# Talking-heads attention with a PReLU layer pair: larger matmul tiles for scores and products, and spaced rows in the relay

## The chip, the cores and the metric

The kernel runs on one core of one Trainium2 chip. The metric is the time of one execution on the device in microseconds (us); lower is better.

## The reference

Four batches, 12 heads, 448 positions, head size 64. The scores are mixed over the heads before the softmax and the weights after it; the result, laid out as 1,792 rows of 768, goes through two dense layers with a PReLU between them. The layers' weights come in as float64.

```python
scores = scale * np.matmul(q, k.transpose(0, 1, 3, 2))
scores = np.einsum('bhij,hg->bgij', scores, w_pre)
attn = np.exp(scores - np.max(scores, axis=-1, keepdims=True))
attn = attn / (np.sum(attn, axis=-1, keepdims=True) + 1e-09)
attn = np.einsum('bhij,hg->bgij', attn, w_post)
x = np.matmul(attn, v)            # then (b, i) rows of 12 x 64
h = x @ w_in
g = np.maximum(h, 0.0) + alpha * np.minimum(h, 0.0)
return g @ w_out
```

## The kernel before

There are two stages. Stage 1 is the attention of all batches; beside it the float64 weights are rounded to float32 on VectorE (`convert`, lines 51 to 57) and stored to memory (`wsc`). Stage 2 (from line 394 on) is the two dense layers: `l1` (line 435) and `l2` (line 460).

In stage 1 the 448 query rows of a batch are cut into four chunks of 110, 110, 110 and 118 rows. A chunk's rows are cut into groups of ten, `GI`, so that ten rows times 12 heads fill 120 partitions; there are 45 groups in a batch and 180 in all. The last group of a 118-row chunk begins two rows early. Two groups make a step `m`; there are 90 steps.

The path of a chunk: `qk` (line 147) computes the scores of two heads, one from the upper and one from the lower 64 rows of the array, on up to 64 query rows at a time, for the six pairs `p` of heads; `qk_out` (line 155) copies them to `s_t`, with the query rows on the partitions and (head, key) along them. `relay` (line 162) is a DMA for each group, on chip: it takes ten rows of `s_t` and lays their 120 (row, head) pairs on 120 partitions of `sr`. `mix` (line 170) multiplies by the pre-softmax weights, `rmax` (175), `exp` (182) and `norm` (188 to 192) make the softmax, and `post` (line 204) applies the post-softmax weights and turns the result, so that keys are on the partitions; `post_out` (214) copies it to `a_t`. When all groups of a chunk are there, `pv` (line 226) multiplies with v, in units of six heads, `hx` 0 and 1. It takes the keys in blocks of 64, seven of them: even blocks from partitions 0 to 63 and odd ones from 64 to 127, each into a PSUM bank of its own, and `pv_out` (235, 236) copies one bank on ScalarE and adds the other on VectorE. The sum is stored to `x2` in memory.

The order on each engine is written out by hand in `step(m)`: the loads that are due, mix(m+1), the stores put off from the step before, the relays (up to those of pair m+4), norm(m-1), rmax(m+1), exp(m), the first `qk` or `pv` unit of this step with its copy, post(m-2), the other units, some of the conversion's operations. [...] Relays are issued in turn from SP and GpSimd. The list `jobs` says at which steps the `qk` and `pv` units and the loads stand, from the groups' numbers. `qk` and `pv` share one PSUM buffer (`ps_s`), `post` has one of its own (`pa`), which is zeroed at the start, and `mix` has two. `sr` has eight buffers, `s_t` two.

Of the kernel before, what the change touches and what calls it, by code (L numbers as in the profile page):

```python
# [14 lines left out]
ALU = mybir.AluOpType  # L15
# [4 lines left out]
B, H, S, D = 4, 12, 448, 64  # L20
DM, DFF = 768, 2048
NT = B * S
GI = 10
GP = GI * H
HI = GI // 2
HP = HI * H
CHUNKS = [(0, 110), (110, 110), (220, 110), (330, 118)]
CW = 118
NCC = DM // 128
NFC = DFF // 128  # L30
NP = H // 2
NS = 4
NJ = S // 64
SR0 = 4
# [26 lines left out]
def talking_heads_prelu(ctx: ExitStack, tc: tile.TileContext, q, k, v, w_pre, w_post, mask, w_in, w_out, alpha, out):  # L61
    nc = tc.nc
# [5 lines left out]
    groups, first = [], []  # L68
    chunk_list = [(b, c) for b in range(B) for c in range(len(CHUNKS))]
    for ci, (b, c) in enumerate(chunk_list):  # L70
        first.append(len(groups))
        cn = CHUNKS[c][1]
        for r in range(0, cn, GI):
            groups.append((ci, min(r, cn - GI)))
    NG, NC = len(groups), len(chunk_list)
    NB = NG // 2
    first.append(NG)
# [34 lines left out]
    k_t, q_t, v_t, s_t, a_t = {}, {}, {}, {}, {}  # L112
# [9 lines left out]
    def load_q(ci, dmas=None):  # L122
        b, c = chunk_list[ci]
        c0, cn = CHUNKS[c]
        q_t[ci] = qp.tile([128, NP, CW], F32, tag="q", name=f"q{ci}")
        for hf in range(2):
            dma = dmas[hf] if dmas else nc.gpsimd
            dma.dma_start(out=q_t[ci][64 * hf:64 * hf + 64, :, :cn],
                          in_=q[b, :, H * c0 + NP * hf * cn:H * c0 + NP * (hf + 1) * cn])

    def load_v(b):
        v_t[b] = vp.tile([128, NS, DM], F32, tag="v", name=f"v{b}")
        nf = S // 128
        nc.gpsimd.dma_start(out=v_t[b][:, :nf, :], in_=v[b, :nf * 128].rearrange("(s p) n -> p s n", p=128))
        nc.gpsimd.dma_start(out=v_t[b][:S - nf * 128, nf, :], in_=v[b, nf * 128:])

    u_t = {}

    def qk(ci, p, ps_pool=None):
        b, c = chunk_list[ci]  # L140
        cn = CHUNKS[c][1]
        ps = (ps_pool or ps_s).tile([128, 2, 512], F32, tag="m" if ps_pool else "s", name=f"s{ci}_{p}")
        for lo in range(0, cn, 64):
            hi = min(lo + 64, cn)
            for hf in range(2):
                r = slice(64 * hf, 64 * hf + 64)
                nc.tensor.matmul(ps[lo:hi, hf, :S], q_t[ci][r, p, lo:hi], k_t[b][r, p, :], start=True, stop=True)  # L147
        u_t["qk", ci, p] = ps

    def qk_out(ci, p, copy=nc.scalar.copy):  # L150
        cn = CHUNKS[chunk_list[ci][1]][1]
        if p == 0:
            s_t[ci] = sp.tile([CW, H, S], F32, tag="s", name=f"st{ci}")
        dst = s_t[ci].rearrange("p (t n) s -> p n t s", t=2)
        copy(dst[:cn, p], u_t.pop(("qk", ci, p))[:cn, :, :S])  # L155

    sr_t, m_t, nm_t, e_t, se_t, r_t = {}, {}, {}, {}, {}, {}

    def relay(n, dma):
        ci, r = groups[n]  # L160
        sr_t[n] = sr_b[n % NSR]
        dma.dma_start(out=sr_t[n][SR0:SR0 + GP], in_=s_t[ci][r:r + GI])  # L162

    def mix(m):

# [41 lines left out]
    def post_out(m):  # L207
        for g in range(2):
            n = 2 * m + g
            ci, r = groups[n]  # L210
            if n == first[ci]:
                a_t[ci] = ap_.tile([128, NS, H, CW], F32, tag="a", name=f"at{ci}")
            dst = a_t[ci].rearrange("p s h i -> p (s h) i")[:, :, r:r + GI]
            nc.scalar.copy(dst, pa[:, g, :NS * GP].rearrange("p (s i) -> p s i", i=GI))  # L214

    def pv(ci, hx, ps_pool=None):
        b, c = chunk_list[ci]
        cn = CHUNKS[c][1]
        ps = (ps_pool or ps_s).tile([128, 2, 512], F32, tag="m" if ps_pool else "s", name=f"x{ci}_{hx}")
        for cl in range(3):  # L220
            for s in range(NS):
                for t in range(2):
                    h = 2 * (3 * hx + cl) + t
                    for r in range(2 if 2 * s + 1 < NJ else 1):
                        pr = slice(64 * r, 64 * r + 64)
                        nc.tensor.matmul(ps[64 * t:64 * t + 64, r, cl * CW:cl * CW + cn], v_t[b][pr, s, h * D:(h + 1) * D],  # L226
                                         a_t[ci][pr, s, h, :cn], start=(s == 0), stop=(2 * s + 2 + r >= NJ))
        u_t["pv", ci, hx] = ps

    def pv_out(ci, hx):  # L230
        b, c = chunk_list[ci]
        c0, cn = CHUNKS[c]
        xe = xep.tile([128, 3, CW], F32, tag="xe", name=f"xe{ci}_{hx}")
        src = u_t.pop(("pv", ci, hx))[:, :, :3 * CW].rearrange("p r (c i) -> p r c i", c=3)
        nc.scalar.copy(xe[:, :, :cn], src[:, 0, :, :cn])
        nc.vector.tensor_tensor(xe[:, :, :cn], src[:, 1, :, :cn], xe[:, :, :cn], ALU.add)  # L236
        later.append(lambda: nc.sync.dma_start(
            out=x2[3 * hx:3 * hx + 3, :, b * S + c0:b * S + c0 + cn].rearrange("c p i -> p c i"), in_=xe[:, :, :cn]))

# [32 lines left out]
    for ci, (b, c) in enumerate(chunk_list):  # L272
        if ci:
            m0, m1 = first[ci - 1] // 2 - RAHEAD, first[ci] // 2 - RAHEAD - 2
            for p in range(NP):
                at(max(m0 + p * (m1 - m0) // (NP - 1), p // 2), "qk", ci, p)
        if ci >= 2:
            at(max(first[ci - 2] // 2 - 1, 0), "load", load_q, ci)
        if c == 0:
            if b:  # L280
                at(first[ci] // 2 - 15, "load", load_k, b)
            at(first[ci] // 2 + 3 if b else 1, "load", load_v, b)
        lb = (first[ci + 1] - 1) // 2
        at(lb + LAG + 1, "pv", ci, 0)
        at(lb + LAG + (3 if ci + 1 < NC else 1), "pv", ci, 1)
    conv_steps = NFC * 2 * 7

    with tc.manual_schedule():
        p0 = ExitStack()
        start = p0.enter_context(tc.tile_pool(name="start", bufs=1))  # L290
        hw = (nc.sync, nc.scalar)
        load_q(0, hw)
        load_k(0, ((0, 1), (1, 3), (3, 6)), hw)

# [18 lines left out]
        for i, w in enumerate((w_pre, w_post)):  # L313
            for p in ((SR0, 64), (0, 64))[i]:
                nc.gpsimd.dma_start(out=mask_sb[p:p + HP, i], in_=mask[:HP, :HI, :])
                nc.gpsimd.dma_start(out=wb[p:p + HP, i, :],
                                    in_=w.rearrange("(o h) g -> o h g", o=1).to_broadcast([HI, H, H]))
        load_q(1)
        nc.gpsimd.dma_start(out=alpha_sb, in_=alpha)
        conv = convert()  # L320
        next(conv)
        nc.vector.scalar_tensor_tensor(
            out=wk[:, :HP].rearrange("p (i g) -> p i g", g=H), in0=mask_sb[:, 0], scalar=scale,
# [4 lines left out]
            out=wq.rearrange("p g i -> p i g"), in0=mask_sb[:, 1],  # L328
# [3 lines left out]
        for p in range(NP):  # L332
            qk(0, p, None if p % 3 == 2 else ps_m)
            qk_out(0, p, nc.vector.tensor_copy if p % 2 else nc.scalar.copy)
# [3 lines left out]
        def relays(upto, dmas):  # L338
            nonlocal relayed
            while relayed < min(upto, NG):  # L340
                relay(relayed, dmas[relayed % len(dmas)])
                relayed += 1

        relays(2 * (RAHEAD + 1), (nc.sync, nc.scalar, nc.gpsimd))
        done = 0
        live = lambda m: 0 <= m < NB
        EV = {"qk": (qk, qk_out), "pv": (pv, pv_out)}

        def step(m):
# [23 lines left out]
            if live(m - LAG):  # L373
                post(m - LAG)
                post_out(m - LAG)
# [52 lines left out]
        def l1(u):  # L428
            b, f = divmod(u, NFC)
            w, x = wi_t.pop(u), xs_t[b]  # L430
            ps = P2["h"].tile([128, 512], F32, tag="h", name=f"h{u}")
            i = 0
            for cc in range(NCC):
                for tw, tx in ((0, 0), (0, 1), (1, 0)):
                    nc.tensor.matmul(ps[:, :S], w[:, tw, cc * 128:(cc + 1) * 128], x[:, tx, cc, :],  # L435
                                     start=(i == 0), stop=(i == 3 * NCC - 1))
                    i += 1
            return ps
# [39 lines left out]
        for u in range(NU + 1):  # L478
            b, f = divmod(u, NFC)
# [4 lines left out]
            if u < NU:  # L484
                split_w(u, 1)
                ps = l1(u)
# [44 lines left out]
```

## Time and profile before

| | us |
|---|---|
| median of 3 runs | 1038.42 |
| lowest, highest | 1031.63, 1039.06 |
| profiled execution, first to last instruction | 1038.9 |

The profiled execution has its span alone; what lies around it is not shown apart. Stage 1 ends, and stage 2 begins, between 540 and 560 us of the span. Rows of the trace begin with a line number of the kernel, the engine and the operation; `out<-in` are the tiles by the program's names: `s` the scores in PSUM, `st` in SBUF, `sr` the relayed rows, `m` the mix, `pa` the output of post, `at` its copy, `x` the products with v, `xe` their copy. Each float32 matmul of the source stands as two in the trace, each with a weight load.

### The profile page before, as it was taken

The page shows a single profiled execution, that of the slowest core. Times are in us where ns is not written, and L with a number is a line of the kernel's source. Part 1 is how long each engine was busy: PE and PEld are TensorE (multiplying, and loading weights), DVE is VectorE, ACT ScalarE, POOL GpSimd, SP SyncE. Part 2 cuts the span into 40 slices and gives each one's busy share as a digit, 9 for nine tenths or more (in the row PEclk, how much of TensorE's full clock was granted, in tenths as well). Part 3 has the DMA queues.
Part 4 walks back from the last instruction along what each step waited for, and adds up shares of the span by engine and source line. Part 5 has one row for each costly group of instructions (what it writes and reads, how often), then busy time and mean ns, then how long its engine had stood idle before and what let it go on. Part 6 is the DMA issues. An engine that isn't in the chain of part 4 may idle for free.

```text
span 1038.9 us, 26286 instructions
## 1 busy us (share of the span) xinstructions
PE 869.1 (84%) x11540; PEld 687.8 (66%) x11540; DVE 500.2 (48%) x886; ACT 441.6 (43%) x870; POOL 348.7 (34%) x305
## 2 busy tenths in 40 slices
PE   4656767867868687778666999999999999999998
PEld 2134444544535355455455999999999999999997
DVE  3454666656657376758624224632265224542222
ACT  1453666655657466648342232323233323232322
POOL 3121222222212122211004455554455454545452
PEclk9687898988889798889796999999999999999999
DMA  7698878897899977898618600020001000010001
GB/s 149 154 185 193 173 190 204 220 220 179 167 228 213 200 191 181 186 247 176 145 32 316 271 1 19 1 89 1 1 19 63 27 1 9 9 54 1 1 1 53
DMA packets 55209, 123.86 MB, mean 119 GB/s; under 512 B 21080, under 2 KB 38840, under 8 KB 54712
## 3 DMA queue, kind: packets, MB, share of 16 engines
q0 software_dynamic: 15232, 59.01, 25.7%
q1 hardware_dynamic: 38546, 60.12, 20.7%
q10 hardware_dynamic: 1318, 3.08, 1.2%
q8 instruction: 90, 1.47, 0.6%
q14 instruction: 23, 0.19, 0.1%
HBM read 59.85 MB, written 23.59 MB: 80 GB/s over the span
## 4 chain that ended last, share of the span: by engine, by line
PE 67%; DMA 16%; ACT 7%; issue 5%; DVE 4%; SPq 1%; POOL 0%; ACTq 0%; DVEq 0%; POOLq 0%
PE h L435 23%; PE acc L460 23%; DMA sr<-st 14%; PE s L147 7%; PE x L226 6%; PE m L170 4%; PE pa L204 4%; ACT st L155 3%; ACT at L214 2%; ACT e L182 1%; DMA xr<-x 1%; DMA wb<-in_w_post_dram 1%; DMA cr<-in_w_out_dram 1%; DVE xe L236 1%; DVE nm L175 1%
## 5 line engine op out<-in xcount | busy, mean ns | idle before, releaser
L435 PE MATMUL h<-xs,wi 128*128 128x448 f32 x1152 | 251.4, 371 | 12.6 <-DVE xs L425 11.3
L460 PE MATMUL acc<-g,wo 128*128 128x448 f32 x1152 | 248.2, 368 | 0.0
L435 PEld LDWEIGHTS h<-xs,wi 128*128 128x128 f32 x1152 | 218.4, 190 | 35.4 <-issue 11.5
L460 PEld LDWEIGHTS acc<-g,wo 128*128 128x128 f32 x1152 | 216.2, 188 | 21.8
L413 POOL TENSOR_TENSOR wi<-wr,wi 128x768 fp32r<-128x768 f32 x64 | 118.6, 1853 | 269.8 <-ACT wi L412 269.8
L204 PEld LDWEIGHTS pa<-r,e 64*64 64x64 f32 x5040 | 115.4, 146 | 79.6 <-issue 55.4
L175 DVE TENSOR_REDUCE nm<-m 128x2 f32<-128x896 f32 x90 | 97.9, 1088 | 135.7 <-PE m L170 135.5
L444 DVE TENSOR_SCALAR t<-h,alpha_sb 128x448 f32<-128x448 f32 x64 | 43.8, 684 | 245.7 <-PE h L435 245.7
L204 PE MATMUL pa<-r,e 64*64 64x60 f32 x5040 | 121.9, 234 | 43.6 <-issue 33.8
L170 PE MATMUL m<-sr,wk 64*64 64x448 f32 (+1 forms) x720 | 111.6, 650 | 50.4 <-DMA sr<-st 43.2
L446 ACT CAST g<-t 128x448 fp32r<-128x448 f32 x64 | 36.3, 567 | 275.2 <-DVE t L445 275.2
L162 POOL DMA_DIRECT2D sr<-st x88 | 54.2, 617 | 276.9 <-PE m L170 185.0
L147 PE MATMUL s<-k,q 64*46 64x448 f32 (+2 forms) x768 | 112.7, 640 | 39.5 <-ACT st L155 27.8
L214 ACT COPY at<-pa 128x480 f32<-128x480 f32 x180 | 93.2, 572 | 82.2 <-PE pa L204 82.0
L413 POOL TENSOR_TENSOR wo<-wr,wo 128x768 fp32r<-128x768 f32 x64 | 123.8, 1935 | 7.6 <-ACT wo L412 5.9
L182 ACT ACTIVATE e<-m,nm 128x448 f32<-128x448 f32 x180 | 113.7, 646 | 14.2 <-DVE nm L175 14.2
L226 PEld LDWEIGHTS x<-at,v 64*64 64x64 f32 x2688 | 88.2, 146 | 37.6 <-issue 20.3
L155 ACT COPY st<-s 110x896 f32<-110x896 f32 (+1 forms) x93 | 84.6, 909 | 63.0 <-PE s L147 55.6
L226 PE MATMUL x<-at,v 64*64 64x110 f32 (+1 forms) x2688 | 92.6, 280 | 18.5 <-issue 13.3
L147 PEld LDWEIGHTS s<-k,q 64*64 64x64 f32 (+2 forms) x768 | 27.5, 140 | 92.3 <-ACT st L155 70.9
L170 PEld LDWEIGHTS m<-sr,wk 64*64 64x64 f32 (+1 forms) x720 | 29.3, 151 | 77.5 <-issue 64.7
L412 ACT CAST wo<-wr 128x768 fp32r<-128x768 f32 x64 | 53.8, 841 | 62.3 <-PE acc L460 62.3
(46 smaller groups left out, 564.1 us busy)
## 6 DMA issues: line engine op xcount, KB each, us to landing
sr<-st SPq DMA_DIRECT2D x89, 210.0 KB
sr<-st POOLq DMA_DIRECT2D x88, 210.0 KB, 9.7
cr<-in_w_in_dram POOLq DMA_DIRECT2D x16, 768.0 KB, 11.5
cr<-in_w_out_dram POOLq DMA_DIRECT2D x16, 768.0 KB, 10.1
wsc<-ct SPq DMA_DIRECT2D x32, 384.0 KB
wr<-wsc SPq DMA_DIRECT2D x14, 768.0 KB
xr<-x SPq DMA_DIRECT2D x24, 224.0 KB
out_dram<-o SPq DMA_DIRECT2D x24, 224.0 KB
```

The costliest lines, as they stand in the source:

```text
L147: nc.tensor.matmul(ps[lo:hi, hf, :S], q_t[ci][r, p, lo:hi], k_t[b][r, p, :], start=True, stop=True)
L155: copy(dst[:cn, p], u_t.pop(("qk", ci, p))[:cn, :, :S])
L162: dma.dma_start(out=sr_t[n][SR0:SR0 + GP], in_=s_t[ci][r:r + GI])
L170: nc.tensor.matmul(ps[hf:hf + 64, u, :S], wk[r, :], g[r, :], start=True, stop=True)
L175: nc.vector.tensor_reduce(out=nm, in_=m_t[m][:, :, :S], axis=AX.X, op=ALU.max, negate=True)
L182: nc.scalar.activation(out=e_t[m][:, u], in_=m_t[m][:, u, :S], func=AF.Exp, bias=nm_t[m][:, u:u + 1], scale=1.0, accum_out=se_t[m][:, u:u ...
L204: nc.tensor.matmul(dst[:, :, HI * u:HI * u + HI], e[h, u, 64 * jb:64 * jb + 64], r[h, u].rearrange("p (h i) -> p h i", h=H), start=True, s ...
L214: nc.scalar.copy(dst, pa[:, g, :NS * GP].rearrange("p (s i) -> p s i", i=GI))
L226: nc.tensor.matmul(ps[64 * t:64 * t + 64, r, cl * CW:cl * CW + cn], v_t[b][pr, s, h * D:(h + 1) * D], a_t[ci][pr, s, h, :cn], start=(s == ...
L413: nc.gpsimd.tensor_tensor(t[:, 1], w, t[:, 0], ALU.subtract)
L435: nc.tensor.matmul(ps[:, :S], w[:, tw, cc * 128:(cc + 1) * 128], x[:, tx, cc, :], start=(i == 0), stop=(i == 3 * NCC - 1))
L460: nc.tensor.matmul(accs[c][:, :S], w[:, tw, c * 128:(c + 1) * 128], g[:, tg], start=(f == 0 and i == 0), stop=(f == NFC - 1 and i == 2))
```

## The change

The chunks are now 120, 120, 120 and 90 rows, the last of which begins at row 358, so that rows 358 and 359 of a batch are in two chunks. A chunk has 12 or 9 whole groups, 45 in a batch as before. A group's ten rows are no longer neighbours: group `r` takes every 12th (9th) row from row `r` on, and writes its ten columns of `a_t` side by side, so that `a_t`'s columns are in the order of the groups. `qk` takes all 120 (90) rows of a chunk in one tile of 64 rows and 128 columns. `pv` takes 128 keys at a time in tiles of 128 rows and 64 columns, four times, into one PSUM bank; the upper half of the last 128 is not there, and v is zero-filled for it (`a_t` has zeros there already). `pv_out` is now three copies on one engine, ScalarE for `hx` 0 and VectorE for `hx` 1, which put the columns back in the order of the rows.

```diff
-CHUNKS = [(0, 110), (110, 110), (220, 110), (330, 118)]
-CW = 118
+CHUNKS = [(0, 120), (120, 120), (240, 120), (358, 90)]
+CW = 120
+QOFF = [H * sum(n for _, n in CHUNKS[:c]) for c in range(len(CHUNKS))]
...
-        cn = CHUNKS[c][1]
-        for r in range(0, cn, GI):
-            groups.append((ci, min(r, cn - GI)))
+        groups += [(ci, r) for r in range(CHUNKS[c][1] // GI)]
...
         nf = S // 128
+        nc.gpsimd.memset(v_t[b][64:, nf, :], 0.0)
...
-        for lo in range(0, cn, 64):
-            hi = min(lo + 64, cn)
-            for hf in range(2):
-                r = slice(64 * hf, 64 * hf + 64)
-                nc.tensor.matmul(ps[lo:hi, hf, :S], q_t[ci][r, p, lo:hi], k_t[b][r, p, :], start=True, stop=True)
+        for hf in range(2):
+            r = slice(64 * hf, 64 * hf + 64)
+            nc.tensor.matmul(ps[:cn, hf, :S], q_t[ci][r, p, :cn], k_t[b][r, p, :], start=True, stop=True)
...
-        dma.dma_start(out=sr_t[n][SR0:SR0 + GP], in_=s_t[ci][r:r + GI])
+        dma.dma_start(out=sr_t[n][SR0:SR0 + GP], in_=s_t[ci][r:CHUNKS[chunk_list[ci][1]][1]:CHUNKS[chunk_list[ci][1]][1] // GI])
...
-            dst = a_t[ci].rearrange("p s h i -> p (s h) i")[:, :, r:r + GI]
+            dst = a_t[ci].rearrange("p s h i -> p (s h) i")[:, :, GI * r:GI * r + GI]
...
-                    for r in range(2 if 2 * s + 1 < NJ else 1):
-                        pr = slice(64 * r, 64 * r + 64)
-                        nc.tensor.matmul(ps[64 * t:64 * t + 64, r, cl * CW:cl * CW + cn], v_t[b][pr, s, h * D:(h + 1) * D],
-                                         a_t[ci][pr, s, h, :cn], start=(s == 0), stop=(2 * s + 2 + r >= NJ))
+                    nc.tensor.matmul(ps[64 * t:64 * t + 64, 0, cl * CW:cl * CW + cn], v_t[b][:, s, h * D:(h + 1) * D],
+                                     a_t[ci][:, s, h, :cn], start=(s == 0), stop=(s == NS - 1))
...
-        src = u_t.pop(("pv", ci, hx))[:, :, :3 * CW].rearrange("p r (c i) -> p r c i", c=3)
-        nc.scalar.copy(xe[:, :, :cn], src[:, 0, :, :cn])
-        nc.vector.tensor_tensor(xe[:, :, :cn], src[:, 1, :, :cn], xe[:, :, :cn], ALU.add)
+        ps = u_t.pop(("pv", ci, hx))
+        copy = nc.vector.tensor_copy if hx else nc.scalar.copy
+        for cl in range(3):
+            copy(xe[:, cl, :cn].rearrange("p (k g) -> p g k", k=GI),
+                 ps[:, 0, cl * CW:cl * CW + cn].rearrange("p (g k) -> p g k", k=GI))
```

The load of q takes its offsets from `QOFF`, since the chunks of q, as laid out for the loads, hold 450 rows a batch.

## Rows read from the trace of the kernel before

**Rows 1.** Stretches: us, busy us (instructions) by engine, granted clock, DMA share, GB/s.

```profile
40.00:520.00 480.00, 352.61 (x8561) 229.47 (x8555) 298.01 (x591) 280.95 (x630) 94.05 (x153) 0.87 0.84 192
540.00:1038.00 498.00, 482.07 (x2388) 437.07 (x2388) 184.31 (x254) 143.16 (x205) 242.17 (x128) 0.98 0.14 50
320.00:360.00 40.00, 28.35 (x675) 17.88 (x669) 23.12 (x48) 20.78 (x46) 7.17 (x12) 0.83 0.98 204
400.00:440.00 40.00, 32.88 (x776) 21.99 (x772) 25.47 (x50) 23.11 (x50) 10.00 (x17) 0.85 0.76 185
160.00:200.00 40.00, 30.06 (x799) 20.20 (x794) 26.08 (x53) 24.70 (x56) 8.87 (x14) 0.91 0.87 221
```

**Rows 2.** The page's chain that ended last, by line, shares of the span.

```profile
PE h L435 23%; PE acc L460 23%; DMA sr<-st 14%; PE s L147 7%; PE x L226 6%; PE m L170 4%; PE pa L204 4%; ACT st L155 3%; ACT at L214 2%; ACT e L182 1%; DMA xr<-x 1%; DMA wb<-in_w_post_dram 1%; DMA cr<-in_w_out_dram 1%; DVE xe L236 1%; DVE nm L175 1%
```

**Rows 3.** The waits of TensorE: us in total, times, longest us.

```profile
PE m L170 <- DMA sr<-st: 43.2, 11, 9.7
PE pa L204 <- issue: 33.8, 14, 6.2
PE s L147 <- ACT st L155: 27.8, 34, 3.2
PE x L226 <- issue: 13.3, 6, 4.9
...
PE m L170 <- issue: 6.2, 2, 3.8
```

**Rows 4.** TensorE in order of time: start, us, ..., [idle before <- releaser].

```profile
14.40 1.72 PE L147 MATMUL s<-k,q 64*64 64x448 f32 x16 [1.31 <-DVE st L155]
16.05 1.27 PE L301 MATMUL warm<-warm 128*128 128x448 f32 x5
...
27.60 3.25 PE L170 MATMUL m<-sr,wk 64*64 64x448 f32 x12 [9.68 <-DMA sr<-st]
33.78 1.01 PE L170 MATMUL m<-sr,wk 64*64 64x448 f32 x2 [2.93 <-DMA sr<-st]
...
359.84 0.40 PE L204 MATMUL pa<-r,e 64*64 64x60 f32 x13 [3.12 <-issue]
...
462.02 0.98 PE L170 MATMUL m<-sr,wk 64*64 64x448 f32 x8 [2.56 <-DMA sr<-st]
462.79 3.98 PE L226 MATMUL x<-at,v 64*64 64x110 f32 x81
...
497.41 1.77 PE L170 MATMUL m<-sr,wk 64*64 64x448 f32 x8 [5.78 <-DMA sr<-st]
...
523.87 2.33 PE L226 MATMUL x<-at,v 64*64 64x110 f32 x81
```

**Rows 5.** The DMA view from 40 to 520 us: all packets, and the instruction queue.

```profile
DMA packets 40872, 92.19 MB, mean 192 GB/s; under 512 B 17077, under 2 KB 27511, under 8 KB 40405
...
q8 instruction: 68, 1.11, 1.0%
```

**Rows 6.** The DMA view from 404.2 to 406.6 us.

```profile
DMA packets 156, 0.25 MB, mean 106 GB/s; under 512 B 17, under 2 KB 152, under 8 KB 156
```

**Rows 7.** The DMA view from 570 to 585 us.

```profile
DMA packets 1337, 6.23 MB, mean 415 GB/s; under 512 B 144, under 2 KB 400, under 8 KB 1336
```

**Rows 8.** Line 162's view: GpSimd's relays, from issue to landing.

```profile
DMA to landing us min/median/max: 5.3/9.7/21.7
```

**Rows 9.** The page's engines, and groups of instructions, shapes kept apart for the copies.

```profile
PE 869.1 (84%) x11540; PEld 687.8 (66%) x11540; DVE 500.2 (48%) x886; ACT 441.6 (43%) x870; POOL 348.7 (34%) x305
...
L147 PE MATMUL s<-k,q 64*46 64x448 f32 (+2 forms) x768 | 112.7, 640 | 39.5 <-ACT st L155 27.8
...
L226 PE MATMUL x<-at,v 64*64 64x110 f32 (+1 forms) x2688 | 92.6, 280 | 18.5 <-issue 13.3
...
L236 DVE TENSOR_TENSOR xe<-x,xe 128x330 f32<-128x330 f32 x24 | 12.0, 500 | 40.6 <-ACT xe L235 40.5
L235 ACT COPY xe<-x 128x330 f32<-128x330 f32 x24 | 10.4, 435 | 53.0 <-PE x L226 53.0
```

More of the change, by code (lines that the diff above doesn't have):

```diff
@@ L128, in load_q @@
             dma.dma_start(out=q_t[ci][64 * hf:64 * hf + 64, :, :cn],
-                          in_=q[b, :, H * c0 + NP * hf * cn:H * c0 + NP * (hf + 1) * cn])
+                          in_=q[b, :, QOFF[c] + NP * hf * cn:QOFF[c] + NP * (hf + 1) * cn])
     def load_v(b):
```

## The prediction

> **What bounds the kernel now.** I took the slowest core's time by stage first, then what each stage waits for, then the transfers behind those waits. The views by stretch [rows 1] split the run in two. From 540 us on TensorE is busy 482 of 498 us at a granted clock of 0.98, in the matmuls of lines 435 and 460, which the diff doesn't touch; the chain of work [rows 2] has 46% of the span there. So everything happens in the first 540 us, and nothing that the change does can give more than that stage has to give.
>
> From 40 to 520 us TensorE is busy 352.6 of 480 us, at a mean clock of 0.87, while the 16 DMA engines are busy 0.84 of the time and yet move only 192 GB/s [rows 1]. The 127 us in which TensorE stands still are told apart by the table of waits [rows 3]: 43.2 us for a relay (the DMA of line 162, s_t to sr) to land, 33.8 + 13.3 + 6.2 = 53.3 us under "issue", in which the profile shows no semaphore that it waited for, and 27.8 us for ScalarE to free the scores' PSUM buffer. VectorE (298 us) and ScalarE (281 us) have slack [rows 1]. The chain gives the relays 14% of the span, the largest share of anything in this stage [rows 2]. So the first stage is TensorE's, held up by transfers.
>
> The "issue" waits I read as late instruction fetches. They break into the middle of a run of post's matmuls, as the 3.12 us at 359.84 [rows 4]; the instruction queue has 68 packets from 40 to 520 us [rows 5], so they would come to 0.8 us a packet; and they are largest where the DMA engines are fullest: the stretch 320 to 360 has a share of 0.98 and that wait is in it, the stretch 400 to 440 has 0.76 and none [rows 1].
>
> **The relay's rate.** Around 405 us one relay runs with almost nothing beside it. It moves 106 GB/s [rows 6]. The same engines move 415 GB/s in the weights' loads of stage 2 [rows 7]: 26 GB/s each. A relay takes ten rows of s_t, so ten engines at that rate would move 260 GB/s. 210 KB are 215,040 B: 2.0 us at the rate shown, 0.83 us at the other, so 1.2 us lie in how it is read or written. The destination is 120 neighbouring partitions before and after; only the source changes, from ten neighbouring partitions to ten that are 12 or 9 apart. The trace alone can't say that the source is the slow side; I take it at the full 1.2 us, between 0 and that, because the destination is spread as widely as that of the fast load. [...]
>
> **The sum, part by part**, against the profiled execution's own span of 1038.9 us, which is 0.5 us over the median of the runs, so no correction is made.
>
> Relay waits. From issue to landing a relay takes 5.3 us at best and 9.7 in the median [rows 8]; the 4.4 between are queueing, mostly behind other relays. With 0.83 for 2.0 us the best becomes 4.1 and the queueing 4.4 x 0.83 / 2.0 = 1.8, together 5.9: every relay lands 3.8 us earlier. Two of the waits are the start's, 9.68 and 2.93 us, with eight relays at once; I leave 5 of the 12.6. The other 30.6 are single waits such as 2.56 and 5.78 us [rows 4], which 3.8 us cover nearly; I leave 3. So 43.2 becomes 8: -35 us (bounds -43 and 0).
>
> Fetch waits. A unit of scores goes from 4 matmuls in the source to 2, one of v's products from 42 to 24. The trace counts two for each: 768 and 2688 become 384 and 1536 [rows 9]. Ahead of stage 2 stand 9,216 matmuls (11,540 less stage 2's 2 x 1,152 and the warm-up's 20), so 1,536 of them go, with as many weight loads: 17%. By count alone the 53.3 us lose 9. With a share of DMA time nearer to 0.65 (92 MB [rows 5] at 415 GB/s would need 222 us, 0.54 of some 410) most fetches come in time: I leave 15, so -38 us (bounds -9 and -53).
>
> Clock. Stalls are followed by work at the lower level: a mix (line 170) takes 1.77 us after the wait at 497.41 and 0.98 at 462.02, and v's products take 3.98 us at 462.79 and 2.33 at 523.87 [rows 4]. I take the mean clock from 0.87 to the 0.91 of the stretch 160 to 200 [rows 1]: 352.6 x (1 - 0.87/0.91) = 15.5 us, of which TensorE's busy share, 0.73, lies on the path: -11 (bounds 0, and -29 at stage 2's 0.98).
>
> Streaming: nothing. Four 64x64 tiles ran side by side, now two larger ones do. Scores: 448 columns by two passes either way, 0.86 us a unit where two stand back to back (1.72 us at 14.40) [rows 4]. v's products: 12 rounds of two either way, 2.33 us for 110 columns; the columns are 450 for 448 in a batch.
>
> Changes of tile shape. All of the stage had 64-row, 64-column tiles; now 96 score units and 32 product units stand between mixes and posts that keep them, so up to 2 x 128 = 256 changes. Between tiles of one shape the next matmul starts 0.21 us ahead of the last one's end (462.02 + 0.98 against 462.79). At the one change of shape in the trace, scores to the warm-up at 16.05, it starts 0.07 ahead of 14.40 + 1.72 [rows 4]. So a change costs between 0 and 0.14 us: 0 to 36. I take half, 18, times 0.73: +13. [...]
>
> Output copies. Before, ScalarE copied one half (435 ns) and VectorE added the other (500 ns) for every unit [rows 9]. Now one engine makes three copies of a third of the columns with a stride in the output, each between 0 and 435 or 500 ns: at most 1.3 us on ScalarE for 16 units (+0.9 each, 14 us) and 1.5 us on VectorE for 16, against what they did for 32. Both have 180 us of slack, and VectorE no longer waits for ScalarE's half. The store that waits for them stands ahead of the relays in SP's queue, as before. If that cover is gone it costs those 14 us; I take 0.
>
> The rest: the memset of v's last half block stands ahead of v's loads and the next relay on GpSimd's queue, four times, some 0.6 us each by the mean of GpSimd's instructions (94 us for 153) [rows 1], and 2 us if it is three times that; v is wanted steps later and the relay three, so 0, at most 8. Rows 358 and 359 of a batch are computed and stored twice; the second store is 9 groups behind the first. The list of steps that holds the jobs has 9 with three or more units (14 before) and 26 with two (20): 0.
>
> Sum: 1038.9 - 35 - 38 - 11 + 13 = 968 us.
>
> **Rivals.** (1) All waits go: -43 - 53 - 29 = 914. For it: a share of 0.76 already had no fetch wait. Against: the in-order handshakes (27.8 us) stay, and faster steps ask for instructions sooner. (2) The waits move: relays come early, but the single PSUM buffer of scores and products, VectorE's conversions and the changes of shape at their full 36 us take their place: 1038.9 - 25 - 25 + 36 - 10 = 1015. (3) The spacing doesn't do what it says, because the ten engines or the destination set the 106 GB/s: what is left is the fetch count, -9, and the changes of shape, +13: 1043, no difference. (4) Slower: two column halves on the same 128 rows don't run side by side. Then a unit takes 4.8 us, not 2.33: 32 x 2.4 = +78 on TensorE itself, with the rest at -65: 1052; it decides as soon as nearly all of the overlap is lost. For it: the trace has no 128-row, 64-column tile. Against: four tiles that shared rows in pairs did run side by side.
>
> **How the numbers follow.** Forecast 0.52; (1) 0.14, reaching up to 940; (2) 0.14; (3) 0.08; (4) 0.12. A measurement of this kernel can tell 1% from no change, so faster by over 1% (below 1028) is 0.80, within 1% 0.08, slower 0.12. The range leaves out (3) and (4): 918 to 1025.
>
> **What would show it.** Right: no wait for a relay over 2 us after the start, a landing near 6 us in the median, a DMA share near 0.65 with more than 192 GB/s, issue waits near 15 us, scores near 0.9 us a unit with four matmuls, products near 2.4 us with 48. Wrong: landings still near 9.7 us (3); products near 4.8 us (4); TensorE waiting for ScalarE or VectorE in place of the relays (2).

## The result and the profile after

The changed kernel takes 950.35 us in the median of 4 runs (945.92 to 958.40), the kernel before 1038.37: a ratio of 0.924, with a 95% interval of 0.913 to 0.935. That is 88 us less; forecast were 71 (968 us, range 918 to 1025). Runs of one kernel lie up to 3% apart: here and below, ratios and intervals come from each kernel's faster runs alone and medians in us from all of them, and the traces of e1 and e3 are of slower runs (1042.2 and 1025.2 us). The profiled execution took 958.4 us, of which 956.1 are its span. The copied lines of code moved: what was L147 is L145, L162 is L160, L170 is L168, L204 is L202 and L226 is L222.

First the stretches of the changed kernel, with the columns of [rows 1].

```profile
40.00:440.00 400.00, 337.33 (x7135) 195.98 (x7136) 289.37 (x594) 275.33 (x639) 96.26 (x155) 0.94 0.81 226
460.00:956.00 496.00, 481.29 (x2352) 436.34 (x2352) 184.03 (x255) 143.04 (x207) 242.22 (x128) 0.99 0.13 50
```

Stage 2 is what it was: 481.3 us of TensorE where [rows 1] has 482.1. All of the gain is in stage 1, where TensorE now stands still for 63 of 400 us (127 of 480 before), at a mean clock of 0.94 in place of 0.87. The rings move 226 GB/s and not 192. The DMA share hardly fell: 0.81 against 0.84.

Next TensorE's waits, as in [rows 3], and one line of ScalarE's.

```profile
PE s L145 <- ACT st L153: 25.9, 15, 11.3
PE m L168 <- DMA sr<-st: 19.2, 7, 6.0
PE pa L202 <- issue: 11.7, 8, 3.9
...
PE x L222 <- issue: 3.5, 1, 3.5
```

```profile
ACT st L153 <- DMA sr<-st: 16.7, 2, 10.2
```

Relay waits went from 43.2 to 19.2 us and issue waits from 53.3 to 15.2. The wait for the scores' PSUM buffer hardly moved in sum, but 11.3 us of it are now one wait: ScalarE stood for 10.2 us before a relay that read the old chunk's rows had landed, and TensorE behind it.

The relay itself: GpSimd's relays from issue to landing, as in [rows 8], and the DMA view from 313.8 to 314.8 us, in which one relay of SP's runs alone (columns of [rows 6], with the rate above them).

```profile
DMA to landing us min/median/max: 2.5/7.3/20.6
```

```profile
GB/s 0 430 72 143 502 72 143 502 72 287 358 72 287 358 143 358 215 143 573 72 143 502 72 215 430 72 287 358 72 358 287 143 358 287 72 144 0 0 0 0
DMA packets 130, 0.22 MB, mean 215 GB/s; under 512 B 10, under 2 KB 130, under 8 KB 130
```

The second fence's first line is the rate in 40 slices of 0.025 us: the relay fills 35 of them, 0.9 us in all, so that the mean over these is some 245 GB/s; forecast were 260 GB/s and 0.83 us. The 106 GB/s of [rows 6] are no fair counterpart. SP had issued two relays for that time, not one (its issues in order of time, before):

```profile
397.08 4.84 SPq L162 DMA_DIRECT2D sr<-st  x2
```

The trace has 135 packets of 1,792 B in that window, and one relay of SP's has 120. Relays that do run alone are set side by side at e6 below.

The two large DMA queues over the whole span (packets, MB, share of 16 engines), before and then after:

```profile
q0 software_dynamic: 15232, 59.01, 25.7%
q1 hardware_dynamic: 38546, 60.12, 20.7%
```

```profile
q0 software_dynamic: 14880, 59.00, 23.0%
q1 hardware_dynamic: 38226, 60.16, 19.4%
```

As time these are 46.4% of 1038.9 us, 482, and 42.4% of 956.1, 405. The engines were relieved of 77 us for the same bytes, while the stage that uses them became 83 us shorter: hence a share that hardly changed.

TensorE in order of time in a stretch without stalls (columns of [rows 4]), and three of the relay waits that are left:

```profile
334.26 0.98 PE L168 MATMUL m<-sr,wk 64*64 64x448 f32 x8
335.33 2.68 PE L222 MATMUL x<-at,v 128*64 128x120 f32 x48
337.94 1.15 PE L202 MATMUL pa<-r,e 64*64 64x60 f32 x56
339.02 1.02 PE L145 MATMUL s<-k,q 64*120 64x448 f32 x4
```

```profile
23.39 3.25 PE L168 MATMUL m<-sr,wk 64*64 64x448 f32 x12 [5.96 <-DMA sr<-st]
27.81 1.76 PE L168 MATMUL m<-sr,wk 64*64 64x448 f32 x4 [1.17 <-DMA sr<-st]
...
63.81 1.77 PE L168 MATMUL m<-sr,wk 64*64 64x448 f32 x8 [4.95 <-DMA sr<-st]
```

A unit of products takes 2.68 us for 120 columns, so the two column halves do run side by side; the estimate for halves that don't was 4.8 us. Where tiles of one shape overlapped by 0.21 us [rows 4], products start 0.09 us behind the end of the mix (334.26 + 0.98), and post starts 0.07 ahead of the end of the products: here a change of shape costs 0.30 us one way and 0.14 the other.

The copies and the memset, as groups with shapes kept apart:

```profile
L233 ACT COPY xe<-x 128x120 f32<-128x120 f32 x36 | 9.8, 417 | 23.8 <-PE x L222 23.8
L233 DVE COPY xe<-x 128x120 f32<-128x120 f32 x36 | 9.7, 374 | 14.5 <-PE x L222 14.5
...
L133 POOL MEMSET v<- 64x768 f32 x4 | 3.3, 818 | 0.0
```

The three copies of a unit take 0.82 us of busy time together. The stride isn't free: e3 below has the same copies without it, at 267 and 275 ns each for 417 and 374. VectorE's 71.6 us of waiting for ScalarE's half are gone; its wait for the products is 14.5 on these.

### The profile page after: what moved, and what is told of

It reads as the page before. It is cut to its first block, busy times and chain, and to the rows that moved or that the text cites. A ratio compares the mean times of both kernels' runs of the same rounds, so it can differ in the third digit from the quotient of the medians.

```text
span 956.1 us, 23286 instructions
## 1 busy us (share of the span) xinstructions
PE 859.1 (90%) x10004; PEld 655.4 (69%) x10004; DVE 496.8 (52%) x902; ACT 438.1 (46%) x886; POOL 352.3 (37%) x309
## 4 chain that ended last, share of the span: by engine, by line
PE 50%; DMA 1%; DVE 0%; issue 0%; SPq 0%; ACT 0%; DVEq 0%; ACTq 0%
PE h L433 25%; PE acc L458 25%; DMA xr<-x 1%; DVE xs L424 0%; PE x L222 0%; SPq L251 0%; DVE xs L423 0%; DVE xe L233 0%; DVE o L462 0%; ACT xe L233 0%; SPq L235 0%; SPq L418 0%; DVEq L423 0%; ACTq L403 0%; DVEq L462 0%
## 5 line engine op out<-in xcount | busy, mean ns | idle before, releaser
L202 PEld LDWEIGHTS pa<-r,e 64*64 64x64 f32 x5040 | 94.8, 137 | 66.5 <-issue 35.6
L160 POOL DMA_DIRECT2D sr<-st x88 | 55.8, 635 | 226.9 <-PE m L168 142.4
L145 PE MATMUL s<-k,q 64*120 64x448 f32 (+1 forms) x384 | 106.7, 630 | 30.3 <-ACT st L153 25.9
L202 PE MATMUL pa<-r,e 64*64 64x60 f32 x5040 | 108.1, 227 | 19.5 <-issue 11.7
L168 PE MATMUL m<-sr,wk 64*64 64x448 f32 x720 | 99.6, 602 | 23.2 <-DMA sr<-st 19.2
L153 ACT COPY st<-s 120x896 f32<-120x896 f32 (+1 forms) x93 | 84.6, 910 | 60.0 <-PE s L145 43.0
L222 PEld LDWEIGHTS x<-at,v 128*64 128x64 f32 x1536 | 74.4, 137 | 31.0 <-ACT at L212 11.3
L222 PE MATMUL x<-at,v 128*64 128x120 f32 (+1 forms) x1536 | 81.9, 262 | 8.2 <-issue 3.5
L145 PEld LDWEIGHTS s<-k,q 64*120 64x120 f32 (+1 forms) x384 | 29.4, 184 | 87.2 <-ACT st L153 61.8
L445 DVE TENSOR_TENSOR g<-t,g 128x448 fp32r<-128x448 f32 x64 | 40.8, 637 | 44.0 <-ACT g L444 44.0
```

Source lines behind the costliest of these rows:

```text
L145: nc.tensor.matmul(ps[:cn, hf, :S], q_t[ci][r, p, :cn], k_t[b][r, p, :], start=True, stop=True)
L160: dma.dma_start(out=sr_t[n][SR0:SR0 + GP], in_=s_t[ci][r:CHUNKS[chunk_list[ci][1]][1]:CHUNKS[chunk_list[ci][1]][1] // GI])
L168: nc.tensor.matmul(ps[hf:hf + 64, u, :S], wk[r, :], g[r, :], start=True, stop=True)
L202: nc.tensor.matmul(dst[:, :, HI * u:HI * u + HI], e[h, u, 64 * jb:64 * jb + 64], r[h, u].rearrange("p (h i) -> p h i", h=H), start=True, s ...
L222: nc.tensor.matmul(ps[64 * t:64 * t + 64, 0, cl * CW:cl * CW + cn], v_t[b][:, s, h * D:(h + 1) * D], a_t[ci][:, s, h, :cn], start=(s == 0) ...
```

## The experiments

My theory: the relays' rate gives most of the gain, by earlier landings and freer rings. Rivals: the larger tiles give it; the new chunks and their steps give it. All kernels here are made from the changed one; the ratios stand against the kernel before on the same chip, and the first four were run together, as were the next four and the last three.

**The parts undone, e1_chunks.** Old tiles, old copies, neighbouring rows; only the chunks and the steps are new.

```diff
-    dma.dma_start(..., in_=s_t[ci][r:CHUNKS[...][1]:CHUNKS[...][1] // GI])
+    dma.dma_start(..., in_=s_t[ci][GI * r:GI * r + GI])
...   # qk, pv and pv_out as before the change, no memset of v
```

> Only the chunks of 120, 120, 120 and 90 rows and the steps that follow from them; a group's ten rows are neighbours and the tiles are 64x64 as before. If the gain comes from the relays' rate and the fetches, as I predicted, nothing changes: 1038 us within 10, a landing near 9.7 us. If the new order of the steps gives it, some 950 to 975.

1039.7 us, ratio 1.0005 (0.994 to 1.007). The new chunks alone do nothing. This kernel's waits (as in [rows 3]) are also the base for the next ones:

```profile
PE m L169 <- DMA sr<-st: 36.7, 10, 13.6
...
PE pa L203 <- issue: 26.6, 13, 4.8
PE x L225 <- issue: 17.5, 7, 5.2
...
PE m L169 <- issue: 5.5, 3, 2.9
```

**Spaced rows alone, e2_spaced.** Old tiles; the two banks of products are put back in order of the rows by VectorE's addition.

```diff
-        copy = nc.vector.tensor_copy if hx else nc.scalar.copy
+        nc.scalar.copy(xg[:, :, :cn], src[:, 0, :, :cn])
         for cl in range(3):
-            copy(xe[...] by (k g), ps[...] by (g k))
+            nc.vector.tensor_tensor(xe[...] by (k g), ps[:, 1, ...] by (g k), xg[...] by (g k), ALU.add)
...   # qk and pv as before the change
```

> The chunks and the rows spaced by 12 or 9, but scores and products on 64x64 tiles as before. By the relays' rate: most of the gain, 960 to 985 us, TensorE's waits for relays near 19 us as with the whole change, the issue waits between 15 and 35 because the instructions are as many as before but the rings are freer. If the tiles and their fewer instructions give the gain: 1025 to 1040, with issue waits still near 53.

994.6 us, ratio 0.965 (0.957 to 0.974): 40 us less than the median of before in this group (1034.99), about half of the whole gain. Its waits:

```profile
PE pa L203 <- issue: 16.6, 10, 3.1
PE m L169 <- DMA sr<-st: 14.4, 4, 5.5
PE x L225 <- issue: 13.9, 8, 4.8
...
PE m L169 <- issue: 4.5, 2, 2.6
```

Against e1 the relay waits fall from 36.7 to 14.4 us, the issue waits only from 49.6 to 35.0, although the rings are as free as with the whole change (397 us of the two large queues, 405 there).

**Larger tiles alone, e3_tiles.** The changed kernel with neighbouring rows.

```diff
-    dma.dma_start(..., in_=s_t[ci][r:CHUNKS[...][1]:CHUNKS[...][1] // GI])
+    dma.dma_start(..., in_=s_t[ci][GI * r:GI * r + GI])
...
-            copy(xe[...] by (k g), ps[...] by (g k))
+            copy(xe[:, cl, :cn], ps[:, 0, cl * CW:cl * CW + cn])
```

> The chunks and the larger tiles, but a group's ten rows are neighbours as before. By the relays' rate: 1025 to 1050 us, since the fetch count gives 9 us and the changes of tile shape take 13 to 36; landing near 9.7 us, relay waits near 43. If the tiles give the gain: 950 to 975.

1017.0 us, ratio 0.976 (0.965 to 0.988): a gain of 2.4%, where I expected none. Its waits:

```profile
PE m L168 <- DMA sr<-st: 67.9, 18, 12.8
...
PE pa L202 <- issue: 11.2, 8, 4.9
PE x L222 <- issue: 3.4, 3, 2.8
...
PE m L168 <- issue: 2.4, 1, 2.4
```

This is the run that teaches most. With rings as full as before (479 us of the two large queues, 482 before), the issue waits fall from e1's 49.6 to 17.0 us, nearly as low as with the whole change: so fewer instructions bring them down even when the rings stay full. But the relay waits rise from 36.7 to 67.9: of 33 us won, 31 come back as waits for relays, which no longer hide behind the other stalls. What e3 still gains lies mostly elsewhere: from 40 us to the end of stage 1 TensorE is busy for 353 us, in e1 for 361.

**The two tile parts apart, e4_spaced_scores and e5_spaced_products.** The changed kernel with the old products (e4), and with the old scores (e5).

```diff
-   (e4) pv and pv_out of the change
+   (e4) pv as before, pv_out as in e2
-   (e5) for hf in range(2): matmul(ps[:cn, hf, :S], q_t[ci][r, p, :cn], ...)
+   (e5) for lo in range(0, cn, 64): for hf in range(2): matmul(ps[lo:hi, hf, :S], q_t[ci][r, p, lo:hi], ...)
```

> Everything but the products, which stay on 64x64 tiles with two PSUM banks, so 32 units fewer change the tile shape and 1,152 more matmuls are to be fetched. If changes of shape cost more than the fetches give: faster than the whole change, 940 to 950 us. If the fetch count matters more: 955 to 970.

981.7 us, ratio 0.944 (0.926 to 0.962); issue waits 35.0 us. The median is slower than the whole change's by more than expected, but the intervals meet.

> Everything but the scores, which stay on 64x64 tiles with four matmuls. The whole change without the products' part gave 981.7 us and with neither part 994.6. If the parts add, this kernel is some 963 us (950 + 13); issue waits near 17 us as with the whole change if it is the products' instructions that made TensorE wait for its instructions.

959.9 us, ratio 0.932 (0.924 to 0.940), issue waits 17.3 us. The products' part carries most of what the tiles give (994.6 to 959.9), the scores' part is within the spread of the runs.

**A spacing of 8, e6_stride8.**

```diff
-    in_=s_t[ci][r:CHUNKS[...][1]:CHUNKS[...][1] // GI]
+    in_=s_t[ci][r % 8:r % 8 + 73:8]
```

> The whole change, but a group takes the ten rows r mod 8, + 8, ... + 72, so rows are relayed more than once and others not at all; all sizes and counts are as in the whole change. [...] If any wide spacing does it: 950 us within 8 and a landing of 7.3.

970.2 us, ratio 0.941 (0.931 to 0.950). The kernel leaves out some rows, so its output is not the reference's; what it moves and computes is as much as in the changed kernel. The relays' landing and TensorE's wait for them:

```profile
DMA to landing us min/median/max: 3.3/7.8/18.2
```

```profile
PE m L168 <- DMA sr<-st: 45.3, 12, 8.7
```

The shortest landing is 3.3 us. In the three kernels with neighbouring rows it is 5.1 to 5.3, in the nine with rows 12 or 9 apart 2.4 or 2.5. The cause is the relay's own time. These are DMA views of three relays, all issued by GpSimd, that run almost alone: neighbouring rows (e3, 298.4 to 302.1 us), rows 8 apart (e6, 309.3 to 311.3) and rows 12 apart (the changed kernel, 205.2 to 206.4).

```profile
DMA packets 99, 0.25 MB, mean 66 GB/s; under 512 B 42, under 2 KB 59, under 8 KB 99
DMA packets 115, 0.29 MB, mean 143 GB/s; under 512 B 44, under 2 KB 74, under 8 KB 114
DMA packets 85, 0.22 MB, mean 185 GB/s; under 512 B 41, under 2 KB 45, under 8 KB 85
```

From the start of its first packet to the end of its last, the relay takes 3.63, 1.86 and 1.00 us in them: 59, 116 and 215 GB/s for the same 215,040 B in the same 40 packets. (The other bytes in the views are not the relay's.)

A spacing of 8 is nearly as wide as one of 9, has the same sizes and counts, and yet its relay takes nearly twice the time: one of GpSimd's relays with rows 9 apart, almost alone in the changed kernel from 422.46 to 423.46 us, takes 1.00 us as well. The relay waits are back at 45.3 us, and the median run is 20 us over the changed kernel's, with intervals that meet. So it isn't any wide spacing that does it: with sizes, counts and destination alike the three times go with the source's partitions, and between 8 and 9 not with how far apart these are. Why ten rows 8 apart take 1.86 us and ten rows 9 apart 1.00 no run shows.

**The form of the copies, e7_chained_copies.**

```diff
-        copy = nc.vector.tensor_copy if hx else nc.scalar.copy
+        nc.scalar.copy(xg[:, :, :cn], ps[:, 0, ...])
         for cl in range(3):
-            copy(xe[...] by (k g), ps[...] by (g k))
+            nc.vector.tensor_tensor(xe[...] by (k g), ps[...] by (g k), xg[...] by (g k), ALU.max)
```

> The whole change, but each unit of products is first copied by ScalarE and then passed through VectorE (a maximum of the PSUM tile with its own copy, so the values stay), which brings back VectorE's wait for ScalarE in every unit. If that wait is what the products' part took away: 965 to 980 us. If it was the instructions: 950 us within 8.

961.6 us, ratio 0.934 (0.927 to 0.942): between the two expectations, and its interval meets the changed kernel's. VectorE waits 51.1 us for ScalarE again, and little or nothing of it reaches the end. Whether the form of the copies gives some us stays open; it isn't the main part.

**More instructions for the same products, e8_halved_products.**

```diff
-        for cl in range(3):
+        for cl, lo in [(cl, lo) for cl in range(3) for lo in (0, cn // 2)]:
+            hi = lo + cn // 2
...
-            nc.tensor.matmul(ps[..., cl * CW:cl * CW + cn], v_t[b][:, s, ...], a_t[ci][:, s, h, :cn], ...)
+            nc.tensor.matmul(ps[..., cl * CW + lo:cl * CW + hi], v_t[b][:, s, ...], a_t[ci][:, s, h, lo:hi], ...)
```

> The whole change, but each matmul of the products is cut into two of half the columns: 3,072 of them in the trace in place of 1,536 (2,688 before), with as much to stream, one tile shape and the same copies. If the count of instructions makes TensorE wait for its instructions: issue waits from 15 back to 35 us or more and 970 to 990 us. If it is something else in the products' part: 950 to 960 us, issue waits near 15.

978.1 us, ratio 0.951 (0.945 to 0.958). Its waits and two units of products:

```profile
PE pa L202 <- issue: 21.6, 12, 3.9
...
PE m L168 <- DMA sr<-st: 14.3, 6, 5.1
...
PE x L223 <- issue: 8.4, 5, 2.9
...
PE m L168 <- issue: 2.2, 1, 2.2
```

```profile
82.85 3.02 PE L223 MATMUL x<-at,v 128*64 128x60 f32 x96
...
157.25 3.00 PE L223 MATMUL x<-at,v 128*64 128x45 f32 x96
```

With 11,540 matmuls in all, as many as before the change, the issue waits are 32.2 us, close to e2's 35.0 with the same count and other tiles. That is over half of the loss, 17 of some 28 us. The rest I had not expected: 96 matmuls take 3.0 us whether they have 60 or 45 columns each, so a unit's time goes by its instructions, at 31 ns each, and 32 units lose some 15 us (24 x 0.34, since 48 matmuls took 2.68, and 8 x 0.92, since 48 of 90 columns took 2.08).

**What holds the changed kernel, e9 to e11.** The changed kernel once more, to compare with (e9); loads behind the relays of their step (e10); and k in three parts besides (e11).

```diff
             relays(2 * (m + 2 + RAHEAD) if m > 2 else first[1], (nc.sync, nc.gpsimd))
+            for f, args in todo:            # e10, e11: moved here from the top of step(m)
+                if f == "load":
+                    args[0](*args[1:])
...
-                at(first[ci] // 2 - 15, "load", load_k, b)
+                for i in range(3):          # e11
+                    at(first[ci] // 2 - 15 + i, "load", load_k, b, ((2 * i, 2 * i + 2),))
```

> The whole change once more, on the same chip as the two that follow, to compare them with: 950 us within 10.

954.1 us, ratio 0.914 (0.904 to 0.925).

> The whole change with one step's loads of q, k and v issued behind its relays and not ahead of them. The largest wait left in the first stage (ScalarE 10.2 us for a relay to land, at 195 us) is a relay that GpSimd issued right behind loads. If its place in that queue makes it late, this wait goes and the time falls by 5 to 15 us; if the rings are full whatever the order, no change within 8.

952.9 us, ratio 0.913 (0.902 to 0.923): no change. ScalarE's long wait for a relay is still there:

```profile
ACT st L153 <- DMA sr<-st: 13.7, 2, 10.0
```

> The one before, and k of a batch comes in three parts in three steps. If it is the size of k's load that relays queue behind, another 3 to 10 us less than that one; if not, the same within 5.

935.8 us, ratio 0.905 (0.899 to 0.911): 18 us under e9 in the median but 9 or 10 by the ratios, as expected, and the intervals meet at 0.904 to 0.911. That wait is 6.7 us now, another one of 9.3 us for a relay has come, and the sum of the relay waits of TensorE is 15.2 us (19.2 in e9). This points to the size of k's load in the rings rather than to the order in GpSimd's queue, without showing it: the gain isn't clear of the noise. It is the fastest kernel of this study in the median.

## Why the prediction was right, point by point

**The bound and the place** were read rightly: nothing changed in stage 2, and stage 1 lost its relay and issue waits and its low clock.

**Relay waits, -35.** Measured -24 (43.2 to 19.2). That the source was the slow side, for the full 1.2 us, was an estimate that no row of before showed; the runs bear it out: e2 took the waits from 36.7 to 14.4, e6 brought them back to 45.3 with nothing but another spacing, and the relays that run alone take 3.63, 1.86 and 1.00 us by their source rows. Two sizes in the sum were wrong. The 2.0 us for a relay were read from a window with two of them; a relay of neighbouring rows alone takes 3.63, so the best landing fell by 2.8 us (5.3 to 2.5) and not by 1.2. And I let all queueing shrink with the relay, from 4.4 to 1.8 us; between the best and the median landing there are still 4.8 us. So the median came to 7.3 us and not 5.9. The two errors pull opposite ways, so the forecast was nearer than its working deserved. The rings also carry the loads of k, q, v and the float64 weights, whose bytes did not change; e11 suggests that k's load alone was worth some 10 us.

**Fetch waits, -38.** Measured -38 (53.3 to 15.2), by a wrong split; that the sums agree is luck. I gave 9 us to the count of instructions and 29 to freer rings, with a DMA share near 0.65, which came out at 0.81. e1 to e3 gives 33 to the count with the rings still full, e1 to e2 gives 15 to the rings with the count still high, and the two overlap. The step that failed is "by count alone the 53.3 us lose 9", which scaled the waits by the count: 17% of stage 1's matmuls went, and two thirds of e1's waits went with them in e3. Why so many stays open. That the waits are largest where the engines are fullest was read from two stretches, and others don't bear it out: 6.9 us from 40 to 80 us at a share of 0.80, 3.2 us from 160 to 200 at 0.87. Shown is that they go with the number of TensorE's instructions (11,540 matmuls: 49.6 us with neighbouring rows, 35.0 and 32.2 with spaced ones; 10,004: 17.0 and 15.2, and between 6 and 19 in the other five kernels with that count).

That these waits are late fetches the prediction only argued; the traces bear it out. Taking all 13 traces from 40 to 545 us, 111 of the 112 issue waits of TensorE that are longer than 1 us end 1.0 to 1.8 us after a packet of the instruction queue has ended; of its 267 other waits of that length 34 do. The wait that ends at 359.84 [rows 4] follows such a packet, from 357.13 to 358.45 us, by 1.4 us. The packets go with the count too, before and then after (91 in e8):

```profile
q8 instruction: 90, 1.47, 0.6%
```

```profile
q8 instruction: 79, 1.29, 0.6%
```

**Clock, -11.** The mean came to 0.94, not 0.91. By the same formula that is 352.6 x (1 - 0.87/0.94) x 0.73 = 19 us. It came with the spacing: from 40 to 440 us the mean is 0.89 in e1 and in e3, and 0.93 in e2. This term and the two before it give 1038.9 - 24 - 38 - 19 = 958; the span is 956.

**Changes of shape, +13.** Those three terms leave nothing for this one. The bound of 0.14 us was too low for one way, 0.30 us from the mix into a larger tile. Yet e5, which takes 192 of the 256 changes away, is not faster; it also brings 384 matmuls back, so it can't tell the two apart. The changes may stand where TensorE would wait for a copy or a landing soon after; no run shows it, and I didn't try a kernel with changes alone.

**Streaming and copies, 0.** Products take 2.68 us where 64x64 tiles take 2.57 for the same 120 columns, some 4 us in all; the copies were free, or nearly (e7).

**The rivals.** (1), all waits gone, went too far: 19 us of relay waits and 15 of issue waits are left, and the clock of 0.94 is nearer to my 0.91 than to its 0.98. (2), the waits move to the PSUM buffer, VectorE and the changes of shape, did not come: the wait for that buffer is 25.9 us, 27.8 before. But waits do move, as e3 shows: issue waits turned into relay waits. Only with both parts is the gain large: spacing alone 3.5%, tiles alone 2.4%, together 7.6% (8.6% in e9). (3) is ruled out by e2 and e6, and (4) by the 2.68 us.

**The signs.** Issue waits near 15 us came, and products (2.68 us) and scores (1.02) were near what was said. Three signs of being right failed: a wait for a relay of 4.95 us stands at 63.81 us, long after the start; the median landing is 7.3 us; the DMA share is 0.81.

## What to carry to other kernels

Two stalls that hide behind each other give little when one is removed (in e3 31 of 33 us came back as waits for relays): judge each part by a run with the other already gone too. Both together can give more than their sum; here it is 7.6 or 8.6% against 5.9, and the difference has a margin of some 1.8 points. For a DMA inside the chip, choose which partitions its few source rows lie on, and time more than one spacing: a relay of ten rows took 3.63 us from neighbouring partitions, 1.86 from partitions 8 apart and 1.00 from 12 or 9 apart. Where small matmuls come in bursts, count TensorE's instructions as a cost of their own (e8, with 1,536 more for the same products, lost some 28 us).

## What the runs showed that I had not expected

A relay alone moves 59 GB/s from ten neighbouring partitions, 116 with a spacing of 8 and 215 with 12 or 9. TensorE's longer waits without a semaphore end 1.0 to 1.8 us after an instruction packet, 111 of 112 of them. Small matmuls in tiles of 128 rows and 64 columns took 31 ns each (96 in 3.0 us, at 60 and at 45 columns). And the DMA engines' busy share stayed at 0.8 while the work on them fell by a sixth (482 to 405 us), because the kernel ran that much faster.
